# Three bursts of small-tile matmuls per batch in an attention and gated feed-forward kernel

## The chip, the cores and the metric

The kernel runs on one core of a Trainium2 chip, as one launch. The metric is the device time in microseconds. Five engines work side by side, each through its own queue in order: TensorE (PE in the profile; its weight loads are shown as PEld), VectorE (DVE), ScalarE (ACT), GpSimd (POOL) and SyncE (SP). They meet only through semaphores. TensorE writes to PSUM, an on-chip memory of eight banks of 2 KB per partition, from which VectorE and ScalarE read; all other operands lie in SBUF. DMAs bring data from and to the main memory (HBM), and some of them transpose within SBUF on the way.

## The reference

There are two stages. The first is an attention over 8 batches, 8 heads, 576 rows and a head width of 64, with 32 packing queries `p` per head; the second is a feed-forward layer with a cosine gate over all 4608 rows of 512.

```python
p_packed = sm_attn(p, k, v)                # 32 rows per head: softmax(scale p k^T) v
out = sm_attn(q, p_packed, p_packed)       # softmax(scale q p_packed^T) p_packed
x = out, heads side by side                # (8*576) x 512
h = x @ w_in                               # 512 x 2048
g = h * cos(h)
result = g @ w_out                         # 2048 x 512
```

The matmuls run in bfloat16 with float32 sums.

## The kernel before, in words

The work is done batch by batch. For a batch `b` the kernel does, in this order:

- `s1`: scores of `p` against `k`, 16 small matmuls (64 rows by 32 columns of the array, form 64*32), and ScalarE's exponentials into `a1`.
- `a1_xbar` (a DMA transpose on SP's queue) or `a1_pe` (TensorE): `a1` transposed into `a1T`, of which there is one buffer.
- `pp`: `a1T` times `v`, 48 small matmuls (form 96*32), copied to `pp_sb` in two copies.
- `pp_T`: two full transposes of `pp_sb` and a copy to `ppT`, the packed keys.
- `ppw` with n = 0 to 3: `ppT` times a quarter of `w_in`, eight small matmuls (64*32) each, copied from PSUM to `PPW`. This folds the second attention's values into `w_in`, so that `h` is computed from the 256 normalised weights `a2n` per row and not from `x`.
- `s2`: scores of `q` against the packed keys (16 small matmuls, 64*32), exponentials into `a2u`; `sums2`: their sums over heads by two full matmuls for each half; `normalise`: `a2n`.
- a slot: 16 steps, one for each 128 columns of `h`. Step `fc` is `h_mm` (four full matmuls of 288 columns, L254), the cosine on ScalarE (`cosT`, L258) and the product on VectorE (`gT`, L261).
- the output: `gT` times `w_out`, 16 matmuls of 512 columns (L342) for each of four chunks of 128 rows, and a fifth chunk (`joint`) for the last 64 rows of two batches; then a copy to `osb` and a store on SP's queue.

The order is written out by hand. The output matmuls of the batch before are the filler: `out_gen` yields after each of them, `fill(n)` issues the next n, so they stand between the dependent pieces and keep TensorE busy while other engines work. `set_filler(b)` (L353) first issues all that is left of the old batch. `slot` (L480) shares out the filler over its 16 steps, by weights, and keeps back `keep` of them; `hooks` are pieces inserted behind a given step, and a step in `heavy` gets half of its larger share ahead of its hook and half behind.

PSUM has three double-bank buffers (`psA`) that all of these share in turn, and two banks (`ot`) for the output. A piece that takes a `psA` buffer waits until the reader of the piece three takes earlier is done. `h_mm` uses 288 of the 512 columns in each bank of its buffer.

In the steady part (batches 3 to 6) the small tiles of a batch come in four bursts: `s2(s)` with `ppw(s, 2)`; `s1(s+1)` with `ppw(s, 3)`; `pp(s+1)` in slot `s` behind step 5, with `pp_T(s+1)` behind step 6; `pw2(s+1)`, that is `ppw(s+1, 0)` and `(s+1, 1)`, behind step 10. Slot 2 has `ppw(2, 2)`, `ppw(2, 3)`, `pp(3)` and `pw2(3)` behind four different steps. Between slots 1 and 2 stand `s1(2)`, `a1_pe`, `pp(2)`, `pp_T(2)`, `s1(3)`, `s2(2)`.

Three queues matter besides TensorE's. SP's queue carries the stores of the output, the transposes of `a1`, `q` and `k`, each in program order. POOL's queue carries the loads of `v`, `q` and `k`; a tiny copy from the transposed `k` (`gate`) ahead of a batch's loads holds them until that transpose has landed. VectorE's and ScalarE's queues are in program order too.

Of the kernel before, what the change touches and what calls it, by code (L numbers as in the profile page):

```python
# [15 lines left out]
def kernel(  # L16
# [15 lines left out]
    NFC = DF // 128  # L32
# [56 lines left out]
    def psa(dt=FP32):  # L89
        return psum["A"].tile([128, 2, 512 if dt == FP32 else 1024], dt, name="psA", tag="A")  # L90
# [104 lines left out]
    def ppw(b, n, eng=None, own=False, later=False, cuts=((0, 512),)):  # L195
        if b not in PPW:
            PPW[b] = ppw_pool.tile([128, 2, DF], BF16, name="PPW", tag="PPW")
        two = isinstance(eng, tuple)
        if own:
            ps = [bank(), bank()]  # L200
        else:
            t = psa()
            ps = [t[:, 0, :], t[:, 1, :]]
        for x in range(4):
            for y in range(2):
                r = slice(64 * y, 64 * y + 64)
                nc.tensor.matmul(ps[y][32 * x:32 * x + 32, :], ppT[b % 2][r, 0, x, :],  # L207
                                 w_in_bf[r, x, n * 512:(n + 1) * 512], start=True, stop=True)

        def evacuate(cuts=cuts):  # L210
            if own or two:
                for a, z in cuts:
                    for y in range(2):
                        copy(eng[y] if two else eng, PPW[b][:, y, n * 512 + a:n * 512 + z], ps[y][:, a:z])
            else:
                copy(eng or (V, ACT)[n % 2], PPW[b][:, :, n * 512:(n + 1) * 512], t)
        if later:
            return [lambda c=c: evacuate((c,)) for c in cuts]
        evacuate()
# [25 lines left out]

    gT, joint = {}, {}

    def h_mm(b, fc):
        if fc == 0:
            g_tile(b)  # L250
        ps = psa()
        for y in range(2):
            for e in range(2):
                nc.tensor.matmul(ps[:, e, 0:HS], PPW[b][:, y, fc * 128:(fc + 1) * 128],  # L254
                                 a2n[b][:, y, e * HS:(e + 1) * HS], start=(y == 0), stop=(y == 1))
        cs = cos_pool.tile([128, S], BF16, name="cosT")
        csv = cs.rearrange("p (e x) -> p e x", e=2)
        ACT.activation(out=csv, in_=ps[:, :, 0:HS], func=AF.Sin, bias=PI_HALF)  # L258

        def rest():  # L260
            V.tensor_tensor(out=gT[b][:, fc, :].rearrange("p (e x) -> p e x", e=2),  # L261
                            in0=ps[:, :, 0:HS], in1=csv, op=ALU.mult)
            if fc % 8 == 7:
                j0 = (b % 2) * 64
                G.tensor_copy(out=joint[b // 2][:, fc - 7:fc + 1, j0:j0 + 64],  # L265
                              in_=gT[b][:, fc - 7:fc + 1, 512:576])
        return rest
# [21 lines left out]
    def h_rest(b):  # L289

        t = psa()
        for fc in range(NFC):
            for y in range(2):
                nc.tensor.matmul(t[:, fc // 8, (fc % 8) * 64:(fc % 8) * 64 + 64],
                                 PPW[b][:, y, fc * 128:(fc + 1) * 128], a2n[b][:, y, 512:576],
                                 start=(y == 0), stop=(y == 1))
        cs = cos_pool.tile([128, 2, 512], BF16, name="cosR", bufs=1)
        ACT.activation(out=cs, in_=t, func=AF.Sin, bias=PI_HALF)
        j0 = (b % 2) * 64
        V.tensor_tensor(out=joint[b // 2][:, :, j0:j0 + 64],  # L300
                        in0=t.rearrange("p a (f x) -> p (a f) x", x=64),
                        in1=cs.rearrange("p a (f x) -> p (a f) x", x=64), op=ALU.mult)
# [16 lines left out]
    def n_chunks(b):  # L319
        return 5 if b % 2 and b < B - 1 else 4  # L320
# [13 lines left out]
    def out_gen(b):  # L334
        groups = [(0, 1), (2,), (3,)] if b == 0 else [(c,) for c in range(n_chunks(b))]
        for grp in groups:
            pss = {c: O.tile([128, DM], FP32, name="ot", tag="ot") for c in grp}
            for f0 in range(0, NFC, 4):
                for c in grp:
                    for fc in range(f0, f0 + 4):  # L340
                        w = joint[b // 2][:, fc, :] if c == 4 else gT[b][:, fc, c * 128:(c + 1) * 128]
                        nc.tensor.matmul(pss[c], w, w_out_bf[:, fc, :],  # L342
                                         start=(fc == 0), stop=(fc == NFC - 1))
                        if fc == NFC - 1:
                            osb = o_pool.tile([128, DM], FP32, name="osb")
                            copy(osb_eng[0], osb, pss[c])
                            for a, z, rows in pieces_of(b, c):
                                nc.sync.dma_start(out=rows, in_=osb[a:z, :])
                        yield

    filler = [None, 0]

    def set_filler(b):  # L353
        fill(1000)
        filler[0] = out_gen(b)
        filler[1] = 16 * n_chunks(b)

    def fill(n):
        while n > 0 and filler[1] > 0:
            next(filler[0])  # L360
            filler[1] -= 1
            n -= 1

    def load_w_in(n):
# [112 lines left out]
    rest_ppw()  # L477
    fill(7)

    def slot(s, hooks, keep=0, heavy={}):  # L480
        left = filler[1] - keep
        weight = [1 + heavy.get(fc, 0) for fc in range(NFC)]
        for fc in range(NFC):
            h_mm(s, fc)()
            quota = (left * sum(weight[:fc + 1])) // sum(weight) - (left + keep - filler[1])
            first = quota
            while hooks and hooks[0][0] == fc:
                if first == quota and fc in heavy:
                    first = quota // 2
                    fill(first)  # L490
                hooks.pop(0)[1]()
            fill(quota - first if first != quota else quota)

    def pw2(b, n=0, eng=None):
        ppw(b, n, eng)
        ppw(b, n + 1, eng)

    def tk(n, b, i):
        return lambda: pe_T(n, b, (ACT, V, ACT), (i,))

    def cross(n, b):
        return lambda: xbar(n, b)

    osb_eng[0] = ACT
    slot(1, [(2, lambda: ppw(1, 2, (ACT, V))), (4, lambda: h_rest(0)),
             (5, lambda: ppw(1, 3, (ACT, V))), (6, lambda: pack_p(2, 4)), (8, tk("k", 2, 0)), (9, tk("k", 2, 1)),
             (9, cross("q", 2)), (10, tk("k", 2, 2)), (12, cross("k", 3))], 4, {4: 2})
    ACT.preload_act_table_set(EXP_SET)
    osb_eng[0] = V
    G.tensor_copy(out=gate, in_=xT["k", 3][0:1, 0, 0:1])  # L510
# [1 line left out]
    load("q", 3)  # L512
    load("k", 4)

    fill(1000)
    set_filler(1)
    s1(2)
    fill(7)
    a1_pe(2, (0,))
# [2 lines left out]
    recips(2)  # L522
    fill(5)
    pp(2)
    fill(2)
    pp_T(2)
    s1(3)
    a1_xbar(3)
    recips(3)
    fill(6)  # L530
    s2(2)
    ppw(2, 0, V)
    xbar("q", 3)
    xbar("k", 4)
    fill(1)
    sums2(2, 0)
    fill(3)
    sums2(2, 1)
# [8 lines left out]
    for n, b in (("v", 4), ("q", 4), ("k", 5)):  # L547
        load(n, b)
    fill(9)
    osb_eng[0] = ACT  # L550
    slot(2, [(3, lambda: ppw(2, 2, (ACT, V))), (6, lambda: ppw(2, 3, (ACT, V))),
             (7, lambda: pp(3, ACT)), (8, lambda: pp_T(3, ACT)), (11, lambda: pw2(3))], 5, {11: 3})

    for s in range(3, B):
        nxt = s + 1 < B
        ACT.preload_act_table_set(EXP_SET)
        osb_eng[0] = V
        fill(1000)
        set_filler(s - 1)
        s2(s)  # L560
        ppw(s, 2, V)
        fill(8)
        if nxt:
            s1(s + 1)
            ppw(s, 3, V)
            a1_xbar(s + 1)
            xbar("q", s + 1)
            recips(s + 1)
            if s + 2 < B:
                xbar("k", s + 2)  # L570
                G.tensor_copy(out=gate, in_=xT["k", s + 2][0:1, 0, 0:1])
        else:
            ppw(s, 3, V)
        fill(4)
        sums2(s, 0)
        fill(5)
        sums2(s, 1)
        normalise(s)
        ACT.preload_act_table_set(SIN_SET)
        fill(13)  # L580
        osb_eng[0] = ACT
        for n, b in (("v", s + 2), ("q", s + 2), ("k", s + 3)):
            if b < B:
                load(n, b)
        slot(s, [(5, lambda: pp(s + 1, ACT)), (6, lambda: pp_T(s + 1, ACT)), (10, lambda: pw2(s + 1))] if nxt else [], 5, {10: 3})
    set_filler(B - 1)
    fill(1000)
    tail_chunk(B - 1, 4)
# [30 lines left out]
```

## Time and profile before

| | |
|---|---|
| median of 3 runs | 249.94 us (249.64 to 250.2) |
| the profiled execution | 249.57 us, its span 247.8 us |
| granted TensorE clock | 0.997 |
| TensorE busy | 238.0 us, 96% |
| ScalarE busy | 170.0 us, 69% |
| VectorE busy | 158.2 us, 64% |
| GpSimd busy | 38.1 us, 15% |
| output matmuls (L342), 512 columns | 560, 380 ns each |
| `h` matmuls (L254), 288 columns | 448, 286 ns each |
| `cosT` (L258), `gT` (L261) | 112 each, 652 and 756 ns |
| PPW copy of 1024 columns | 1222 ns on VectorE, 1012 ns on ScalarE |
| transposed `a1` by DMA | 5, from issue to landing 3.9 to 13.9 us |

The span runs from the first to the last instruction; the time of the execution holds 1.8 us more around it. The length of one matmul is longer than the distance between the starts of two, because matmuls are pipelined: sums are made with the distances. An engine is idle where its next instruction waits, and the profile names what ended last. The slots lie at about 40 to 62 us (slot 1), 75 to 94 (2), 104 to 120 (3), 129 to 148 (4), 158 to 173 (5), 183 to 201 (6) and 211 to 225 (7).

### The profile page before, as it was taken

The numbers are of one execution on the slowest core, as the hardware profiler recorded it, in microseconds if no ns is written. First come the engines' busy times: TensorE is split into PE (matmuls) and PEld (weight loads), VectorE is DVE, ScalarE is ACT, GpSimd is POOL, SyncE is SP. The second block draws the span as 40 slices with busy tenths as digits, with TensorE's granted clock in tenths as the row PEclk, the third lists the DMA queues.
The fourth block names the chain that finished last, engine by engine and source line by source line (L and its number), as shares of the span: only waits on it lengthen the run. The fifth ranks groups of instructions, "written<-read, shape, count | busy, mean of one in ns | idle before, by whom it ended". The sixth has DMA issues, their size and how long they took to land.

```text
span 247.8 us, 5456 instructions
## 1 busy us (share of the span) xinstructions
PE 238.0 (96%) x2239; PEld 128.3 (52%) x2239; DVE 158.2 (64%) x244; ACT 170.0 (69%) x284; POOL 38.1 (15%) x61
## 2 busy tenths in 40 slices
PE   7999899999999899999999999999999999999993
PEld 3463344566435554565446554565456554665452
DVE  3369987676449677578757666578756685774000
ACT  2359998667477777888787677977886685874110
POOL 8532320200130032004100500030000000000000
PEclk9999999999999999999999999999999999999998
DMA  6999999998799989996999796979592113111123
GB/s 91 205 209 209 202 207 228 198 238 144 160 128 184 201 188 186 213 208 170 177 177 233 128 228 143 176 148 182 115 184 62 42 45 84 43 33 54 52 75 85
DMA packets 63992, 37.37 MB, mean 151 GB/s; under 512 B 36592, under 2 KB 59376, under 8 KB 63968
## 3 DMA queue, kind: packets, MB, share of 16 engines
q0 software_dynamic: 23184, 18.81, 50.1%
q1 hardware_dynamic: 40624, 18.09, 35.5%
q8 instruction: 17, 0.28, 0.5%
q10 hardware_dynamic: 160, 0.13, 0.2%
q14 instruction: 7, 0.06, 0.1%
HBM read 37.22 MB, written 9.44 MB: 188 GB/s over the span
## 4 chain that ended last, share of the span: by engine, by line
PE 80%; ACT 5%; DVE 4%; issue 1%; DVEq 0%; ACTq 0%
PE ot L342 48%; PE psA L254 21%; PE psA L207 3%; PE psA L137 2%; ACT cosT L285 2%; PE psA L233 2%; DVE gT L286 1%; PE ot L328 1%; PE psA L180 1%; DVE PPW L87 1%; ACT cosT L258 1%; DVE gT L261 1%; ACT a2u L225 1%; DVE joint L300 0%; PE psA L192 0%
## 5 line engine op out<-in xcount | busy, mean ns | idle before, releaser
L342 PE MATMUL ot<-w_out_bf,gT 128*128 128x512 bf16 x512 | 133.2, 380 | 0.0
L261 DVE TENSOR_TENSOR gT<-psA,cosT 128x576 bf16<-128x576 f32 x112 | 83.5, 756 | 33.2 <-ACT cosT L258 32.2
L258 ACT ACTIVATE cosT<-psA 128x576 bf16<-128x576 f32 x112 | 72.9, 652 | 26.7 <-PE psA L254 25.3
L254 PE MATMUL psA<-a2n,PPW 128*128 128x288 bf16 x448 | 73.3, 286 | 0.1
L342 PEld LDWEIGHTS <-gT 128*128 128x128 bf16 x512 | 47.2, 98 | 43.4 <-issue 7.8
L254 PEld LDWEIGHTS <-PPW 128*128 128x128 bf16 x448 | 43.8, 98 | 30.8 <-issue 1.2
L87 DVE CAST PPW<-psA 128x1024 bf16<-128x1024 f32 (+1 forms) x25 | 26.1, 1048 | 6.8 <-PE psA L207 6.8
L87 DVE COPY osb<-ot 128x512 f32<-128x512 f32 (+1 forms) x14 | 9.4, 670 | 21.3 <-PE ot L328 17.4
L85 ACT COPY osb<-ot 128x512 f32<-128x512 f32 (+1 forms) x23 | 13.2, 576 | 13.5 <-PE ot L342 12.4
L265 POOL COPY joint<-gT 128x512 bf16<-128x512 bf16 x14 | 8.6, 616 | 85.3 <-DVE gT L261 85.2
L243 DVE SCALAR_TENSOR_TENSOR a2n<-a2u,r,lns 128x576 bf16<-128x576 bf16 x16 | 12.4, 813 | 8.2 <-ACT lns L241 8.2
L146 ACT ACTIVATE a<-psA 128x576 bf16<-128x576 f32 x16 | 10.3, 646 | 8.3 <-PE psA L137 8.3
L235 ACT ACTIVATE lns<-psA 128x576 f32<-128x576 f32 x16 | 10.3, 650 | 6.5 <-PE psA L233 5.9
L342 PE MATMUL ot<-w_out_bf,joint 128*128 128x512 bf16 x48 | 12.8, 379 | 0.0
L225 ACT ACTIVATE a2u<-psA,rs 128x576 bf16<-128x576 f32 x16 | 11.0, 736 | 1.0 <-PE psA L137 0.9
L379 PE MATMUL ot<-wz 128*128 128x512 bf16 (+1 forms) x17 | 9.0, 639 | 1.9 <-DVE wz L393 1.7
L207 PE MATMUL psA<-w_in_bf,ppT 64*32 64x512 bf16 x224 | 10.4, 380 | 0.0
L241 ACT ACTIVATE lns<-lns 128x576 f32<-128x576 f32 x16 | 10.0, 673 | 0.0
L286 DVE TENSOR_TENSOR gT<-psH,cosT 128x512 bf16<-128x512 f32 x15 | 9.3, 681 | 0.4 <-ACT cosT L285 0.4
L85 ACT CAST PPW<-psA 128x1024 bf16<-128x1024 f32 (+1 forms) x9 | 7.4, 826 | 2.9 <-PE psA L207 2.8
L285 ACT ACTIVATE cosT<-psH 128x512 bf16<-128x512 f32 x15 | 8.4, 627 | 0.7 <-DVE gT L286 0.6
L280 PE MATMUL psH<-a2n,PPW 128*128 128x512 bf16 x30 | 7.8, 382 | 0.8 <-DVE PPW L87 0.8
(94 smaller groups left out, 167.3 us busy)
## 6 DMA issues: line engine op xcount, KB each, us to landing
kbf<-in_k_dram POOLq DMA_DIRECT2D x8, 576.0 KB, 13.7
vbf<-in_v_dram POOLq DMA_DIRECT2D x8, 576.0 KB, 8.0
qbf<-in_q_dram POOLq DMA_DIRECT2D x8, 576.0 KB, 11.1
out_dram<-osb SPq DMA_DIRECT2D x24, 192.0 KB, 3.0
out_dram<-osb SPq DMA_DIRECT2D x22, 128.0 KB, 2.6
w_in_bf<-in_moe_w_in_dram POOLq DMA_DIRECT2D x4, 512.0 KB, 16.5
w_out_bf<-in_moe_w_out_dram POOLq DMA_DIRECT2D x4, 512.0 KB, 21.3
out_dram<-osb SPq DMA_DIRECT2D x26, 64.0 KB, 2.1
```

The costliest lines, as they stand in the source:

```text
L85: ACT.copy(out=out, in_=in_)
L87: eng.tensor_copy(out=out, in_=in_)
L146: ACT.activation(out=a1[b % 2][:, y, :, 0:TP].rearrange("p (e m) x -> p e m x", e=2), in_=ps[y][:, :, 0:HS].rearrange("p e (m x) -> p e m ...
L207: nc.tensor.matmul(ps[y][32 * x:32 * x + 32, :], ppT[b % 2][r, 0, x, :], w_in_bf[r, x, n * 512:(n + 1) * 512], start=True, stop=True)
L225: ACT.activation(out=a2u[b][:, y].rearrange("p (e x) -> p e x", e=2), in_=ps[y][:, :, 0:HS], func=AF.Exp, scale=rs1[b][:, y:y + 1])
L243: V.scalar_tensor_tensor(out=a2n[b][:, y], in0=a2u[b][:, y], scalar=r1[b][:, y:y + 1], in1=lns[b][:, y], op0=ALU.mult, op1=ALU.mult)
L254: nc.tensor.matmul(ps[:, e, 0:HS], PPW[b][:, y, fc * 128:(fc + 1) * 128], a2n[b][:, y, e * HS:(e + 1) * HS], start=(y == 0), stop=(y == 1))
L258: ACT.activation(out=csv, in_=ps[:, :, 0:HS], func=AF.Sin, bias=PI_HALF)
L261: V.tensor_tensor(out=gT[b][:, fc, :].rearrange("p (e x) -> p e x", e=2), in0=ps[:, :, 0:HS], in1=csv, op=ALU.mult)
L285: ACT.activation(out=cs, in_=ps, func=AF.Sin, bias=PI_HALF)
L286: return lambda: V.tensor_tensor(out=gT[b][:, fc, 0:512], in0=ps, in1=cs, op=ALU.mult)
L342: nc.tensor.matmul(pss[c], w, w_out_bf[:, fc, :], start=(fc == 0), stop=(fc == NFC - 1))
```

## The change

- In slot 1 `ppw(1, 2)` and `ppw(1, 3)` stand together behind step 2 (`pw2`), no longer behind steps 2 and 5; five outputs, not four, stand on each side of `h_rest`.
- `pp(2)` and `s1(3)` stand together, `pp_T(2)` behind them after three outputs; the outputs around `s2(2)` and `sums2(2)` are spread anew.
- In slots 2 to 6 one hook remains, `tiled(s)`, behind step 6 (slot 2) or 5: `ppw(s, 2)`, `ppw(s, 3)` and `pp(s+1)` in one burst. `pp` writes its 128 columns into the spare columns of the step's own buffer (`spare`); its copies, and those of `ppT`, go to VectorE. Most of the step's outputs stand ahead of the burst, three behind.
- `ppw(s, 0)` and `ppw(s, 1)` move from the slot before to `s2(s)` and `s1(s+1)`; for the last batch `ppw` 1 to 3 stand together.
- `pp_T(s+1)` moves behind the last step's `h_mm`, ahead of that step's `gT`.
- The filler becomes a list: what a slot leaves over (5, 10 or 13 outputs) is no longer issued at once but goes on ahead of the next batch's; so odd and even batches get about the same number of outputs per slot.

```diff
     def h_mm(b, fc):
         if fc == 0:
             g_tile(b)
         ps = psa()
+        spare[0] = ps[:, 1, HS:512]
...
-    filler = [None, 0]
+    filler = []
 
     def set_filler(b):
-        fill(1000)
-        filler[0] = out_gen(b)
-        filler[1] = 16 * n_chunks(b)
+        filler.append([out_gen(b), 16 * n_chunks(b)])
...
-    def slot(s, hooks, keep=0, heavy={}):
-        left = filler[1] - keep
-        weight = [1 + heavy.get(fc, 0) for fc in range(NFC)]
+    def slot(s, hooks, keep=0, heavy={}, last=None):
+        left = to_do() - keep
+        weight = [1 + heavy.get(fc, (0, 0))[0] for fc in range(NFC)]
         for fc in range(NFC):
-            h_mm(s, fc)()
...
+            rest = h_mm(s, fc)
+            if fc == NFC - 1 and last:
+                last()
+            rest()
+            quota = (left * sum(weight[:fc + 1])) // sum(weight) - (left + keep - to_do())
+            behind = min(quota, heavy[fc][1]) if fc in heavy else quota
+            fill(quota - behind)
             while hooks and hooks[0][0] == fc:
...
                 hooks.pop(0)[1]()
+            fill(behind)
...
+    def tiled(b):
+        own, later = spare[0], []
+        for n in (2, 3):
+            later += ppw(b, n, (ACT, V)[n - 2], later=True)
+        later[0]()
+        pp(b + 1, V, own=lambda: own)
+        later[1]()
...
-    slot(1, [(2, lambda: ppw(1, 2, (ACT, V))), (4, lambda: h_rest(0)),
-             (5, lambda: ppw(1, 3, (ACT, V))), (6, lambda: pack_p(2, 4)), ...], 4, {4: 2})
+    slot(1, [(2, lambda: pw2(1, 2, (ACT, V))), (4, lambda: h_rest(0)), (6, lambda: pack_p(2, 4)),
+             ...], 4, {2: (1, 2), 4: (3, 5)})
...
     pp(2)
-    fill(2)
-    pp_T(2)
     s1(3)
     a1_xbar(3)
+    fill(3)
+    pp_T(2)
     recips(3)
-    fill(6)
+    fill(5)
     s2(2)
...
-    slot(2, [(3, lambda: ppw(2, 2, (ACT, V))), (6, lambda: ppw(2, 3, (ACT, V))),
-             (7, lambda: pp(3, ACT)), (8, lambda: pp_T(3, ACT)), (11, lambda: pw2(3))], 5, {11: 3})
+    slot(2, [(6, lambda: tiled(2))], 10, {6: (5, 3)}, lambda: pp_T(3, V))
...
         s2(s)
-        ppw(s, 2, V)
+        ppw(s, 0, V)
         fill(8)
         if nxt:
             s1(s + 1)
-            ppw(s, 3, V)
+            ppw(s, 1, V)
...
         else:
-            ppw(s, 3, V)
-        fill(4)
+            for n in range(1, 4):
+                ppw(s, n, V)
+        fill(4 if nxt else 6)
...
-        slot(s, [(5, lambda: pp(s + 1, ACT)), (6, lambda: pp_T(s + 1, ACT)), (10, lambda: pw2(s + 1))] if nxt else [], 5, {10: 3})
+        if nxt:
+            slot(s, [(5, lambda: tiled(s))], 5 if s % 2 else 13, {5: (5, 3)}, lambda: pp_T(s + 1, V))
+        else:
+            slot(s, [], 5)
```

More of the change, by code (lines that the diff above doesn't have):

```diff
@@ L246 @@
     gT, joint = {}, {}
+    spare = [None]
     def h_mm(b, fc):
@@ L349, in out_gen, with to_do @@
                         yield
-    filler = [None, 0]
+    filler = []
     def set_filler(b):
-        fill(1000)
-        filler[0] = out_gen(b)
-        filler[1] = 16 * n_chunks(b)
+        filler.append([out_gen(b), 16 * n_chunks(b)])
+    def to_do():
+        return sum(n for _, n in filler)
     def fill(n):
-        while n > 0 and filler[1] > 0:
-            next(filler[0])
-            filler[1] -= 1
+        while n > 0 and filler:
+            next(filler[0][0])
+            filler[0][1] -= 1
+            if filler[0][1] == 0:
+                filler.pop(0)
             n -= 1
@@ L478, with pw2 @@
     fill(7)
-    def slot(s, hooks, keep=0, heavy={}):
-        left = filler[1] - keep
-        weight = [1 + heavy.get(fc, 0) for fc in range(NFC)]
+    def slot(s, hooks, keep=0, heavy={}, last=None):
+        left = to_do() - keep
+        weight = [1 + heavy.get(fc, (0, 0))[0] for fc in range(NFC)]
         for fc in range(NFC):
-            h_mm(s, fc)()
-            quota = (left * sum(weight[:fc + 1])) // sum(weight) - (left + keep - filler[1])
-            first = quota
+            rest = h_mm(s, fc)
[5 more added lines that the diff above has]
+            fill(quota - behind)
             while hooks and hooks[0][0] == fc:
-                if first == quota and fc in heavy:
-                    first = quota // 2
-                    fill(first)
                 hooks.pop(0)[1]()
-            fill(quota - first if first != quota else quota)
-    def pw2(b, n=0, eng=None):
+            fill(behind)
+    def pw2(b, n, eng=None):
         ppw(b, n, eng)
         ppw(b, n + 1, eng)
+    def tiled(b):
[5 more added lines that the diff above has]
+        later[1]()
     def tk(n, b, i):
@@ L504 @@
     osb_eng[0] = ACT
-    slot(1, [(2, lambda: ppw(1, 2, (ACT, V))), (4, lambda: h_rest(0)),
-             (5, lambda: ppw(1, 3, (ACT, V))), (6, lambda: pack_p(2, 4)), (8, tk("k", 2, 0)), (9, tk("k", 2, 1)),
-             (9, cross("q", 2)), (10, tk("k", 2, 2)), (12, cross("k", 3))], 4, {4: 2})
+    slot(1, [(2, lambda: pw2(1, 2, (ACT, V))), (4, lambda: h_rest(0)), (6, lambda: pack_p(2, 4)), (8, tk("k", 2, 0)), (9, tk("k", 2, 1)),
+             (9, cross("q", 2)), (10, tk("k", 2, 2)), (12, cross("k", 3))], 4, {2: (1, 2), 4: (3, 5)})
     ACT.preload_act_table_set(EXP_SET)
@@ L513 @@
     load("k", 4)
-    fill(1000)
     set_filler(1)
+    fill(4)
     s1(2)
@@ L534 @@
     xbar("k", 4)
-    fill(1)
+    fill(3)
     sums2(2, 0)
@@ L557 @@
         osb_eng[0] = V
-        fill(1000)
         set_filler(s - 1)
+        fill(5)
         s2(s)
-        ppw(s, 2, V)
+        ppw(s, 0, V)
         fill(8)
```

## The prediction

> **What bounds the kernel now.** I read the page's busy line and its chain first, then TensorE's timeline, then the DMA rows of one tile. The page:
>
> ```profile
> span 247.8 us, 5456 instructions
> PE 238.0 (96%) x2239; PEld 128.3 (52%) x2239; DVE 158.2 (64%) x244; ACT 170.0 (69%) x284; POOL 38.1 (15%) x61
> ...
> PE 80%; ACT 5%; DVE 4%; issue 1%; DVEq 0%; ACTq 0%
> ```
>
> TensorE is the bound and no other engine is near it. So the change must be priced in TensorE's time: what its instructions cost each other, and its waits. Starts of equal neighbours give the first: an output matmul (L342, 512 columns) follows the next by 0.216 us, an L254 (288 columns) by 0.122, so one step of a slot (four L254) is 0.49 us. The timeline of TensorE shows what a burst of small tiles adds (columns: start, length, work):
>
> ```profile
> 140.48 1.24 PE L342 MATMUL ot<-w_out_bf,gT 128*128 128x512 bf16 x5
> 141.66 0.62 PE L207 MATMUL psA<-w_in_bf,ppT 64*32 64x512 bf16 x16
> 142.21 0.61 PE L342 MATMUL ot<-w_out_bf,gT 128*128 128x512 bf16 x2
> ```
>
> Five outputs from 140.48 end their turns at 141.56; the burst starts at 141.66, an entry of 0.093 (the same for every burst that waits for nothing). From there to the next output are 0.558 us for 16 small matmuls, and 0.342 for eight (82.14 to 82.48). So eight cost 0.216 and leaving costs 0.126; the output after a burst is 0.010 late. One burst costs 0.093+0.126+0.010 = 0.229 us beyond its own matmuls. From 35 us on there are 31.
>
> The other cost is waiting. Gaps beyond these starts, added up: slot 1 0.30 and 0.18 (49.1 and 50.0, the buffer of h_rest) and 0.33 (53.9); before slot 2 0.05, 0.08 and 0.38; slot 2 0.15, 0.09 and 0.89; slots 3 and 5 0.35 each; slots 4, 6 and 7 none. The largest stands ahead of pp(3):
>
> ```profile
> 82.93 0.65 PE L254 MATMUL psA<-a2n,PPW 128*128 128x288 bf16 x4
> 84.40 0.56 PE L180 MATMUL psA<-vbf,a1T 96*32 96x64 bf16 x48 [0.82 <-DVE PPW L87]
> 84.89 0.60 PE L342 MATMUL ot<-w_out_bf,gT 128*128 128x512 bf16 x2
> ```
>
> The row blames VectorE, but the rows of a1T between 60 and 90 us name the last arrival:
>
> ```profile
> L160 SPq DMA_TRANSPOSE a1T<-a x1: 4630/4630/4630, 70.5 to 70.5; - x1
> its engine sat idle before it (us, times) until:
> ...
>   DMA a1T<-a: 1.1, 1
> ...
> DMA to landing us min/median/max: 13.9/13.9/13.9
> ```
>
> Issued at 70.45, landed 13.91 later at 84.36: pp(3) waits for a DMA, which TensorE's savings do not speed up. The sum is therefore split there.
>
> **Up to pp(3).** Slot 1: one burst joined (ppw 2 and 3), -0.229. With five outputs instead of four behind h_rest and no ppw ahead of pack_p, I count 0.06+0.06 left of 0.30+0.18, and 0.37 instead of 0.33 at the second kT transpose (its buffer still waits for ScalarE's 0.80 copy). s1(2) comes at 62.46 instead of 63.01.
>
> pp(2) then starts at 66.85 and issues its 48 in 0.358. s1(3) behind it would start at 67.2, but needs kT(3), whose transpose landed at 67.46 after a chain of loads that TensorE does not pace. I take 67.50 (was 68.67). It ends after 0.381; three outputs 0.648, pp_T 0.112 (its pp_sb was ready at 67.8), five outputs 1.08 and an entry put s2(2) at 69.81 (was 70.44). Three outputs instead of one cover a2u, which needs 1.18 after s2's start: 0.60+0.65 = 1.25, so the 0.38 goes. Slot 2 begins at 75.02 (was 75.57, with two outputs fewer done).
>
> In slot 2 VectorE is late: after a2n it still has two PPW copies and an osb, ending 1.98 after the slot's start, and the first gT is done at +2.64. With 1, 1, 2 outputs step 3 wants its buffer at +2.33: a wait of 0.36. Step 6 comes at +5.03, its own 0.49, six outputs 1.30, an entry 0.093 and sixteen ppw 0.432 later pp(3) wants to start: 75.02+5.03+2.31 = 82.36, say 82.45 with the change of shape below.
>
> Its a1T is issued 1.78 after s1(3), at 69.3 instead of 70.45, and now ahead of two output rows on SP's queue. In the trace's packets nothing of the SP queues moves from 69 to 73 us, while the loads of batches 3 and 4 start; then come the output rows; a1T's packets run from 74.9, one for one with the loads', 185 per us, about 100 per us beside output rows. There are 1536. Starting at 73 they are through by 82; starting 1.1 earlier than now, by 83.2. Landing between 82.2 and 83.3; I take pp(3) at 82.9. The bounds are 82.45 (no wait) and 84.40 (as now). The two output rows go out some 4.6 us later; four osb buffers of about 3.5 us each cover that. The gain here: 84.40-82.9 = 1.50.
>
> **From pp(3) on.** By then the new kernel has done three outputs more (0.65) and one step less (0.49): 0.16. The burst of ppw(3) in slot 2 is gone: 0.229. Slots 3 to 6 have one burst less each, but in the joined one the ppw tiles (64*32) meet those of pp (96*32). No row shows such a meeting. M, its cost, lies between 0 (s2 into ppw, both 64*32: 371+342-588 ns is the 0.125 of one exit) and 0.229 (as if the burst had been left). I take 0.1, the half that an entry is: 4 x (0.229-0.1) = 0.52. (The same meetings in slot 2 and at s1(3) hide under the two DMA waits.)
>
> The Trainium skill speaks against the joining: TensorEngine Tiling (Array Packing), Key Properties, says that a change of tiling mode, not of the tile alone, drains TensorE. It gives no figure; by it a joined burst of two shapes is still two drains, and were a drain a whole exit and entry, the 0.52 would be 0.
>
> The waits of slots 3 and 5 go (0.35+0.35): pp moves into the step's own buffer, pp_T to the slot's end. New there: pp_T takes the buffer of step 13, freed 2.2 us after that step's start (cosT 0.65, gT 0.76 and their starts), and wants it at 2.0 to 2.3: 0.19 in slot 2, 0.08 in slot 3. Net -0.43.
>
> What I cost at nothing, with its cover. The new step 6 shares its buffer with pp: pp ends 0.56 after its start, VectorE's two pp_sb copies take 0.42 more, and the step starts 0.49+0.01+0.65 after pp: some 0.13 spare, given by the three outputs behind the burst. If VectorE is late by x there, x is paid in five slots. PPW 3, behind pp_sb on VectorE (1.22), is done at 2.2 and needed at 3.0. pp itself waits for the step's gT, 2.3 after the step's start at worst; it wants to start at 2.3 (slot 3) to 2.7. ppT (0.29 on VectorE, ahead of the last gT) has 1.6 us until s2. pp_sb and ppT leave ScalarE, which is not the bound. In slot 7 three PPW copies of 1.22 queue on VectorE behind an osb: done 4.3, 5.5 and 6.6 after s2's start; sums2 wants the first two buffers at 4.5 and 5.8, step 0 the third at 8.9. POOL's queue keeps its order. a1T(4) landed at 108.15 for a pp(4) at 108.78; the new pp(4) is due near 107.6, and its a1T is issued 3 us earlier: 0 to 0.5, taken as 0.
>
> **Sum.** 1.50+0.16+0.23+0.52+0.43 = 2.84 us off the profiled execution's 249.57 us: 246.7. The runs shown have a median of 249.94, 0.37 above it, so 247.1.
>
> **The rivals.** (a) a1T(3) lands as now, at 84.4: the loads, not its issue, set it. For it: it landed 0.2 after kbf's load (84.16). Then only what follows pp(3) is gained, 1.34: 248.6. (b) No drain between small shapes and a1T in time: 0.45+0.40 more: 246.2. (c) The change of shape costs a whole burst, M = 0.23, and VectorE's slack of 0.13 at pp_sb is gone: -0.52 and some 0.2 in each of four slots: 248.4; with (a) 249.9, no change. (d) Slower: M beyond 0.81, in slots 3 to 6 (2.84+0.40 over four); at M = 1.0 the time is 250.7. For it only that no row shows the meeting; against it that no entry, exit or entry of 96*32 from 128*128 (0.093) is over 0.13. That the change does not do what it says is excluded by the order of TensorE's instructions: 22 bursts from 35 us on, not 31.
>
> **How the numbers follow.** Forecast 246.5 to 247.7: 0.50. (a) 0.22, (b) 0.11, (c) alone 0.08, both 0.04, (d) 0.05. 247.1 is the likeliest. The range from 246.0 to 248.9 takes in (b), (a) and (c), and leaves out 1 in 10. Within 0.2% (0.5 us, about what a measurement here can tell) is (c) with (a). Faster 0.90, same 0.05, slower 0.05.
>
> **What would show it.** Right: 22 bursts; pp behind ppw starting 0.43+M after it (M read directly); pp(3) between 82.4 and 83.3; a1T(3) issued near 69.3; no gap at the step after pp; slots 3 and 5 without gaps. Wrong: pp(3) still at 84.4; M over 0.2; gaps at the step behind pp with VectorE's pp_sb as releaser; a wait of sums2 in slot 7; new waits for a1T in slots 3 to 6.

## The result, and the profile after

The changed kernel takes 247.46 us (median of 17 runs, 246.26 to 250.19) against 249.78 us (17 runs) for the kernel before: a ratio of 0.9907, 95% interval 0.9891 to 0.9923, that is 2.3 us gained (1.9 to 2.7) where 2.84 were forecast. The profiled execution took 247.53 us against 249.57. (The ratios leave out executions more than 1.5% above the fastest of their kernel, which are one of the changed kernel's (250.19 us), one of run 3's (254.87) and three of run 9's six (251 to 255); what made them long was not traced.)

The first lines of the page, and its chain by engine:

```profile
span 245.7 us, 5424 instructions
PE 232.0 (94%) x2204; PEld 128.4 (52%) x2239; DVE 162.4 (66%) x259; ACT 166.6 (68%) x267; POOL 38.1 (16%) x61
...
PE 80%; DMA 13%; ACT 2%; issue 2%; DVE 1%; DVEq 0%
```

TensorE is still the bound, but the chain now holds 13% of DMA. About 7% is the first load of `q`; 6% is this transfer, as the rows of `a1T` between 60 and 90 us have it (operation, its issue; then from issue to landing):

```profile
L160 SPq DMA_TRANSPOSE a1T<-a x1: 4942/4942/4942, 69.2 to 69.2; - x1
...
DMA to landing us min/median/max: 14.4/14.4/14.4
```

and here is what waits for it, on TensorE's timeline of slot 2:

```profile
81.86 0.63 PE L207 MATMUL psA<-w_in_bf,ppT 64*32 64x512 bf16 x16
83.68 0.56 PE L180 MATMUL psA<-vbf,a1T 96*32 96x64 bf16 x48 [1.20 <-DMA a1T<-a]
84.39 0.59 PE L345 MATMUL ot<-w_out_bf,gT 128*128 128x512 bf16 x2 [0.16 <-issue]
```

pp(3) came at 83.68 instead of 84.40, a gain of 0.72. TensorE was ready for it 1.2 us earlier: it had been made faster than the transfer. (The last row's 0.16 is no wait: an output matmul is missing from the records there, as in all bursts marked so.)

The other reading is the meeting of the two small shapes, in slot 4, where nothing waits for a DMA:

```profile
134.13 0.62 PE L207 MATMUL psA<-w_in_bf,ppT 64*32 64x512 bf16 x16
134.68 0.55 PE L180 MATMUL psA<-vbf,a1T 96*32 96x64 bf16 x48
...
135.83 0.65 PE L257 MATMUL psA<-a2n,PPW 128*128 128x288 bf16 x4
```

Sixteen ppw take 0.432; pp starts 0.55 after the first of them. The meeting costs M = 0.12. It is the same in slots 3, 5 and 6. From 35 us on there are 22 bursts, as forecast, where there were 31. After pp(3) TensorE's last matmul comes 157.79 later, before it was 159.07: 1.28 gained there (forecast 1.34).

So two things had to be tried: whether 0.12 is really the price of a change of shape, and what makes a1T(3) land so late.

### The profile page after: what moved, and what is told of

It reads as the page before. It is cut to its first block, busy times and chain, and to the rows that moved or that the text cites. A ratio compares the mean times of both kernels' runs of the same rounds, so it can differ in the third digit from the quotient of the medians.

```text
span 245.7 us, 5424 instructions
## 1 busy us (share of the span) xinstructions
PE 232.0 (94%) x2204; PEld 128.4 (52%) x2239; DVE 162.4 (66%) x259; ACT 166.6 (68%) x267; POOL 38.1 (16%) x61
## 4 chain that ended last, share of the span: by engine, by line
PE 80%; DMA 13%; ACT 2%; issue 2%; DVE 1%; DVEq 0%
PE ot L345 45%; PE psA L257 21%; DMA qbf<-in_q_dram 7%; DMA a1T<-a 6%; PE ot L385 3%; PE psA L207 2%; PE psA L137 2%; PE psA L180 1%; PE ot L331 1%; PE psA L233 1%; PE psA L112 1%; ACT kT L85 1%; ACT a L146 1%; PE psA L192 0%; PE psA L170 0%
## 5 line engine op out<-in xcount | busy, mean ns | idle before, releaser
L345 PE MATMUL ot<-w_out_bf,gT 128*128 128x512 bf16 x483 | 127.3, 379 | 2.5 <-issue 2.1
L264 DVE TENSOR_TENSOR gT<-psA,cosT 128x576 bf16<-128x576 f32 x112 | 83.3, 757 | 19.5 <-ACT cosT L261 18.5
L345 PEld LDWEIGHTS <-gT 128*128 128x128 bf16 x512 | 48.1, 98 | 39.8 <-issue 4.4
L87 DVE CAST PPW<-psA 128x1024 bf16<-128x1024 f32 (+1 forms) x25 | 26.9, 1092 | 6.6 <-PE psA L207 6.4
L345 PE MATMUL ot<-w_out_bf,joint 128*128 128x512 bf16 x47 | 12.0, 380 | 0.2
L385 PE MATMUL ot<-wz 128*128 128x512 bf16 (+1 forms) x15 | 8.3, 660 | 2.0 <-DVE wz L399 1.7
L85 ACT CAST PPW<-psA 128x1024 bf16<-128x1024 f32 (+1 forms) x7 | 6.1, 891 | 5.8 <-PE psA L207 5.8
L207 PE MATMUL psA<-w_in_bf,ppT 64*32 64x512 bf16 x224 | 9.8, 379 | 0.0
L588 POOL COPY gate<-kT 1x1 bf16<-1x1 bf16 x3 | 0.5, 181 | 50.8 <-DMA kT<-kbf 50.8
## 6 DMA issues: line engine op xcount, KB each, us to landing
kbf<-in_k_dram POOLq DMA_DIRECT2D x8, 576.0 KB, 13.7
```

The costliest lines, as they stand in the source:

```text
L85: ACT.copy(out=out, in_=in_)
L87: eng.tensor_copy(out=out, in_=in_)
L345: nc.tensor.matmul(pss[c], w, w_out_bf[:, fc, :], start=(fc == 0), stop=(fc == NFC - 1))
L385: nc.tensor.matmul(wps, w[:, 0:128], w, start=True, stop=True)
```

## The experiments

All are edits of the changed kernel, each compared with the kernel before on its own chip. Since the first 35 us differ by up to 1.0 us from execution to execution, traces are compared from the start of s2(1) to the last matmul of TensorE ("from s2(1)"). Each row's last five columns are those of one traced execution. "Held" marks the runs whose loads wait until a1T(3) has landed.

| kernel | median us | ratio to before, 95% | from s2(1) | a1T(3), issue to landing | v(3)'s load issued ahead of a1T(3) by | a1T(3) lands behind k(4)'s load by | pp(3) waits for a1T(3) |
|---|---|---|---|---|---|---|---|
| before | 249.78 | | 208.35 | 13.91 | 2.70 | 0.20 | 0.82 |
| changed | 247.46 | 0.9907 (0.9891–0.9923) | 206.30 | 14.41 | 1.61 | 0.69 | 1.20 |
| 1 shapes mixed | 252.58 | 1.0108 (1.0078–1.0139) | 211.15 | 13.53 | 1.98 | 0.19 | 0.54 |
| 2 bursts apart | 248.07 | 0.9918 (0.9887–0.9949) | 206.81 | 13.90 | 2.12 | 0.72 | 0.62 |
| 3 loads behind a1T(3) | 252.53 | 1.0096 (1.006–1.0132) | 211.19 | 4.31 | held | | 0 |
| 4 outputs ahead | 246.78 | 0.9887 (0.9861–0.9912) | 205.31 | 14.67 | 1.54 | 0.66 | 0 |
| 5 four more | 248.62 | 0.9962 (0.9944–0.9981) | 207.60 | 14.60 | 1.54 | 0.35 | 0.52 |
| 6 six ahead | 246.81 | 0.9885 (0.9858–0.9913) | 205.29 | 12.83 | 2.96 | 0.43 | 0 |
| 7 behind two a1T | 254.46 | 1.0193 (1.0146–1.0241) | 212.14 | 4.33 | held | | 0 |
| 8 unequal outputs | 247.06 | 0.9903 (0.9872–0.9933) | 205.43 | 11.58 | 3.45 | 0.62 | 0 |
| 9 behind all a1T | 249.14 | 0.9886 (0.985–0.9922) | 205.19 | 4.61 | held | | 0 |
| 10 one behind | 248.59 | 0.9957 (0.993–0.9984) | 206.51 | 11.40 | 3.69 | 0.58 | 0 |
| 11 own buffer | 247.62 | 0.992 (0.9889–0.9952) | 206.95 | 13.94 | 2.03 | 0.66 | 0.73 |
| 12 three waits covered | 246.15 | 0.9881 (0.9856–0.9907) | 204.59 | 12.81 | 2.25 | 0.35 | 0 |

### What a change of shape costs: runs 1 and 2

Run 1 mixes the shapes, with `pp` cut into four pieces of twelve matmuls (its loop yields after every third `j`) and a piece taken after every four ppw:

```diff
-        for n in (2, 3):
-            later += ppw(b, n, (ACT, V)[n - 2], later=True)
+        small = pp(b + 1, V, own=lambda: own, parts=True)
+        for n in (2, 3):
+            later += ppw(b, n, (ACT, V)[n - 2], later=True, between=small)
...
+            if between is not None and x % 2:
+                next(between)
```

> The burst of slots 2 to 6 with the same 64 matmuls in another order: four of ppw, twelve of pp, and so on, so that the two shapes meet seven times and not once. Theory (every meeting of the two shapes costs TensorE 0.12 us, read from pp's start 0.55 after ppw's in the changed kernel): the burst of slots 3 to 6 grows from 1.05 to 1.77 us, 4 x 0.72 = +2.9; in slot 2 the wait for a1T(3) now comes after four ppw, so twelve ppw and six meetings, 1.0, lie behind it: +3.9 us in all, about 251.4. Rival (the 0.12 is one short wait of pp, for its buffer or its data, and not paid for each meeting): bursts as long as now, only slot 2 loses the twelve ppw, +0.3, 247.8.

TensorE's timeline of slot 4:

```profile
136.26 0.40 PE L215 MATMUL psA<-w_in_bf,ppT 64*32 64x512 bf16 x4
136.59 0.27 PE L186 MATMUL psA<-vbf,a1T 96*32 96x64 bf16 x12
136.79 0.40 PE L215 MATMUL psA<-w_in_bf,ppT 64*32 64x512 bf16 x4
137.12 0.27 PE L186 MATMUL psA<-vbf,a1T 96*32 96x64 bf16 x12
```

Each meeting is paid anew, in both directions. Twelve pp are a quarter of 0.358, 0.09, and the ppw behind them starts after 0.20: 0.11. The rival is dead. But a slot grew by 1.07 (from one s2 to the next 27.58 instead of 26.51), not 0.72. The four ppw show why: pp starts 0.33 behind them. With a meeting of 0.115, that is 0.216 for four, what eight take when they stand together. (In the changed kernel, too, pp starts 0.33 behind the second eight ppw, and these start 0.23 behind the first eight.) So cutting a group of eight in half saves nothing, and four half groups cost 0.43 in place of the reckoned 0; with six more meetings at 0.11 it is 1.1.

Run 2 takes the bursts apart. The edit moves three outputs from ahead of the burst to between ppw and pp; the three behind stay, unlike in the expectation, so that its wait of step 6 could not arise (run 10 has it).

```diff
-            fill(quota - behind)
+            fill(quota - behind - (3 if s >= 2 and fc in heavy else 0))
...
         later[0]()
+        fill(3)
         pp(b + 1, V, own=lambda: own)
```

> The changed kernel with the three outputs that stand behind ppw 2 and 3 and pp put between ppw and pp, in slots 2 to 6: bursts apart again, nothing else moved. Theory (a meeting costs 0.12, an exit and an entry 0.229): +0.11 in each of slots 3 to 6, and step 6 behind pp then wants its buffer 0.65 earlier, while pp_sb is ready 0.1 before it now: a wait of some 0.55 more in each, +2.6 in all; in slot 2 the outputs hide under the wait for a1T(3). Rival 1 (pp_sb is not what step 6 waits for): +0.4. Rival 2 (a meeting costs as much as a burst): no change, if the buffer is no limit either.

```profile
133.74 0.63 PE L207 MATMUL psA<-w_in_bf,ppT 64*32 64x512 bf16 x16
134.30 0.82 PE L345 MATMUL ot<-w_out_bf,gT 128*128 128x512 bf16 x3
135.05 0.56 PE L180 MATMUL psA<-vbf,a1T 96*32 96x64 bf16 x48
...
136.20 0.65 PE L257 MATMUL psA<-a2n,PPW 128*128 128x288 bf16 x4
```

From the burst's start to step 6 are 2.46, of which 0.648 are the three outputs between: 1.81 against 1.70 (134.13 to 135.83 above). Apart costs 0.11 a slot, as 0.229 less 0.12 says. So joining two shapes saves half of a burst, not a whole one and not nothing. Slots 4 to 6 lost 0.11 each; slot 3 lost more only because a1T(4) landed later in this execution (108.54).

### What makes a1T(3) late: runs 3, 5, 7 and 9

Run 3 holds the three loads that are issued just ahead of a1T(3) until it has landed:

```diff
-    load("v", 3)
-    load("q", 3)
-    load("k", 4)
...
     a1_xbar(3)
+    G.tensor_copy(out=gate, in_=a1T[3][0:1, 0, 0, 0:1])
+    load("v", 3)
+    load("q", 3)
+    load("k", 4)
```

> The loads of v(3), q(3) and k(4) are held on GpSimd's queue until a1T(3) has landed; in the changed kernel they are issued just ahead of it. Theory (a1T(3) lands 14.4 us after its issue because its packets take turns with those of the loads; alone the transposes of a1 of slots 5 and later take 4 to 5): a1T(3) lands near 74, pp(3) starts at 82.4 and not 83.68, 1.28 us gained there; v(3) lands near 80, in time. The loads of batch 4 then come some 3 to 5 us later and a1T(4) shares with them: it may land up to 4 late for pp(4) at 108.3. So 246.2 if a1T(4) is in time, up to 250 if not; in either case pp(3) at 82.4. Rival (the transfer is slow by itself, as the landing of a1T(3) was moved by 0.73 for an issue 1.23 earlier): pp(3) still at 83.5 or later, 247.5 or more.

The rows of `a1T`, first between 60 and 90 us, then between 92 and 125:

```profile
L160 SPq DMA_TRANSPOSE a1T<-a x1: 1437/1437/1437, 69.6 to 69.6; - x1
...
DMA to landing us min/median/max: 4.3/4.3/4.3
```

```profile
L160 SPq DMA_TRANSPOSE a1T<-a x1: 4815/4815/4815, 97.7 to 97.7; - x1
...
DMA to landing us min/median/max: 14.3/14.3/14.3
```

The theory holds: without the loads the transfer takes 4.3 us, and pp(3) starts 0.63 after its burst, with no wait for it. That is 0.08 more than in slots 4 to 6, because here the step's gT is late on VectorE: in runs 3, 8, 9 and 10 pp(3) starts 0.05 us behind the end of that gT. The same meeting then takes place one batch later, between a1T(4) and the loads that now come behind. This agrees with the Trainium skill, DMA: Bandwidth & Descriptors, Queues, rings and completion order: a DMA engine takes the queues that have work in turn, a packet at a time. In the trace of the changed kernel a1T's packets of 256 bytes run one for one with the loads' of 768, some 175 to 195 of each per us from 75 to 80 us.

That also tells when it lands. These are the rows of k(4)'s load, the last of the three, in the changed kernel and then in run 8 (see below), whose program is the same up to there:

```profile
L94 POOL DMA_DIRECT2D kbf<-in_k_dram x1: 772/772/772, 69.1 to 69.1; - x1
...
DMA to landing us min/median/max: 13.8/13.8/13.8
```

```profile
L94 POOL DMA_DIRECT2D kbf<-in_k_dram x1: 769/769/769, 67.7 to 67.7; - x1
...
DMA to landing us min/median/max: 12.9/12.9/12.9
```

In the changed kernel k(4) landed at 82.94 and a1T(3) at 83.63, in run 8 at 80.55 and 81.17. By the table a1T(3) landed 0.2 to 0.7 behind k(4) in all eleven executions where the loads run beside it, and was the longer under way the less the loads were ahead of it: 14.4 to 14.7 with v(3) issued 1.5 to 1.6 ahead, 11.4 and 11.6 with 3.7 and 3.5. The loads themselves go 0.3 after kT(3) has landed (at 67.33 and 65.85 here). That the landing follows the loads is read from these rows; only their removal was tried.

What followed was dearer than the wait. TensorE's timeline, and the windows of the same core (busy time of PE, PEld, DVE, ACT, POOL; then the granted clock):

```profile
106.96 0.62 PE L207 MATMUL psA<-w_in_bf,ppT 64*32 64x512 bf16 x16
112.08 0.83 PE L180 MATMUL psA<-vbf,a1T 96*32 96x64 bf16 x48 [4.50 <-DMA a1T<-a]
...
114.10 1.17 PE L257 MATMUL psA<-a2n,PPW 128*128 128x288 bf16 x4
```

```profile
107.00:112.00 5.00, 0.58 (x17) 0.09 (x16) 0.32 (x1) 1.01 (x1) 0.00 (x0) 0.98 1.29 178
112.00:115.50 3.50, 3.08 (x56) 1.96 (x58) 1.55 (x3) 0.20 (x1) 0.00 (x0) 0.54 1.19 154
115.50:120.00 4.50, 4.50 (x33) 2.94 (x31) 3.37 (x5) 3.86 (x7) 1.96 (x4) 1.00 0.91 221
```

After 4.5 us without work TensorE got half its clock. From s2(3) to s2(4) this kernel took 31.93, the changed one 25.93: 6.0, of which only 4.6 are the wait.

Run 7 also holds q(4) and k(5) behind a1T(4):

```diff
             a1_xbar(s + 1)
+            if s == 3:
+                G.tensor_copy(out=gate, in_=a1T[4][0:1, 0, 0, 0:1])
+                load("q", 4)
+                load("k", 5)
```

> The loads of v(3), q(3), k(4) behind the landing of a1T(3), as before, and now those of q(4) and k(5) behind the landing of a1T(4), with v(4) left ahead of it. Theory (each late a1T is late by the loads that it shares the DMA engines with, and no longer when they stand behind it): pp(3) at 82.4 without a wait; a1T(4), issued at 97.7, shares with v(4) alone and lands by 105, ahead of pp(4) at 107; q(4) and k(5) land near 110 and 114, in time: 1.28 gained on the changed kernel, 246.2. Rival (a transfer held back is late for its own reader): a wait at s2(4), s1(5) or pp(5) near 120 to 133, 246.8 to 249.

a1T(4) landed at 103.67, 5.4 after its issue, and pp(4) had no wait: right for the two that were freed. But neither theory nor rival had what came next. Batch 5's loads, issued from 119.8, met a1T(5), issued at 122.96, which took this long:

```profile
L160 SPq DMA_TRANSPOSE a1T<-a x1: 4911/4911/4911, 123.0 to 123.0; - x1
...
DMA to landing us min/median/max: 14.8/14.8/14.8
```

pp(5) waited 4.1 us, the clock was 0.51 for the six us behind it, and slot 4 was 7.0 longer (33.54 against 26.52).

Run 9 holds them in every batch: the edit of run 7 without its `if`, and only `v(s+2)` loaded ahead of the slot.

> As the two runs with loads held back, now for every batch: v(s+2) is loaded ahead as before, q and k behind the landing of that batch's a1T. The first held back one batch's loads and a1T(4) landed 14.3 us after its issue, the second two and a1T(5) landed 14.8 after: the meeting moved on by a batch each time. Theory (a1T is slow whenever three loads run beside it and takes 4 to 6 us beside none or one): all five land within 7 us of their issue, no pp waits, pp(3) at 82.4, and nothing else moves: 1.28 gained on the profiled execution of the changed kernel, 246.2. Rival (q and k are then late): waits of s2 or s1 in slots 5 to 7, over 247.

The five transfers landed 4.6, 6.0, 6.6, 6.1 and 7.7 after their issue, no pp waited, and the span from s2(1) was 205.19. So the mechanism is shown in every batch. Its last transfer took 0.7 longer than expected. As a kernel it is not to be had: half of its executions were 4 to 9 us longer. The loads of `q` and `k` now start some 13 us later, and their margins are thin (kT(6) landed at 146.44 for an s1(6) at 147.95); one that misses its reader would do that, but no such execution was traced, so the cause is open.

Run 5 asks whether the wait is TensorE's own. Four more output matmuls, whose result is not used, are put ahead of the burst in slot 2 and behind that of slot 4:

```diff
+                        if (b, c, fc) in ((1, 3, 0), (3, 3, 0)):
+                            for _ in range(4):
+                                nc.tensor.matmul(pss[c], w, w_out_bf[:, fc, :], start=True, stop=True)
                         nc.tensor.matmul(pss[c], w, w_out_bf[:, fc, :],
```

> Four more output matmuls (each a sum of its own into the bank that the chunk's first matmul then starts anew), 4 x 0.216 = 0.86 us of TensorE, at two places: in slot 2 just ahead of the burst with pp(3), and in slot 4 just behind the burst with pp(5). Theory (pp(3) waits 1.28 us for the landing of a1T(3), slot 4 has no wait): slot 2 absorbs its four, pp(3) still at 83.6 to 83.7 and slot 3 begins when it did; slot 4 pays 0.86 in full: +0.86 in all, 248.3. Rival (the 1.28 are paced by VectorE or by TensorE's own order, as the row ahead of the change blamed VectorE): pp(3) at 84.5, +1.7, 249.2.

```profile
80.59 1.03 PE L347 MATMUL ot<-w_out_bf,gT 128*128 128x512 bf16 x4
...
82.84 0.63 PE L207 MATMUL psA<-w_in_bf,ppT 64*32 64x512 bf16 x16
83.99 0.56 PE L180 MATMUL psA<-vbf,a1T 96*32 96x64 bf16 x48 [0.52 <-DMA a1T<-a]
```

Slot 2 swallowed most of its four: the burst came 0.98 later than in the changed kernel, pp(3) only 0.31, and that much later a1T(3) had landed (83.94 against 83.63). From one s2 to the next slot 2 grew by 0.20, slot 4 by 27.38 less 26.52 = 0.86, which is four starts of 0.216. With 0.24 lost ahead of s2(2), where s1(3) waited for kT(3), that is the 1.30 from s2(1). pp(3) is not paced by TensorE's own order, and VectorE, which the row of the kernel before blamed, is not what it waits for.

### Filling the wait: runs 4 and 6

```diff
-    slot(2, [(6, lambda: tiled(2))], 10, {6: (5, 3)}, lambda: pp_T(3, V))
+    slot(2, [(6, lambda: tiled(2))], 1, {6: (13, 3)}, lambda: pp_T(3, V))
...
-            slot(s, [(5, lambda: tiled(s))], 5 if s % 2 else 13, {5: (5, 3)}, lambda: pp_T(s + 1, V))
+            slot(s, [(5, lambda: tiled(s))], {3: 2, 4: 13, 5: 5, 6: 13}[s], {5: (5, 3)}, lambda: pp_T(s + 1, V))
```

That is run 4, which also has `fill(4)` and `fill(2)` around `sums2(1, 0)` and `(1, 1)` in place of 2 and 1. Run 6 has 4 and `{6: (10, 3)}` in slot 2 and leaves the start as it was.

> More outputs ahead of pp(3): slot 2 keeps 1 instead of 10 and sets the nine more of them ahead of its burst; slots 3 to 6 keep 2, 13, 5, 13; and four and two outputs instead of two and one stand around sums2 of batch 1, ahead of slot 1. Theory (pp(3) waits for the landing of a1T(3) at 83.6, whatever TensorE does before, so work moved ahead of it is free; the 1.2 us of waiting there hold five to six outputs of 0.216, and the three at the start cover part of the waits ahead of slot 1): 1.2 to 1.6 us gained, 245.9 to 246.3. Rival (the wait moves along with the work, as other engines pace it): no change, 247.5.

> The run with outputs set ahead of the wait again, without its three at the start and with six instead of nine in slot 2: slot 2 keeps 4 and not 10, slots 3 to 6 keep 2, 13, 5, 13. Theory: six of 0.216 are 1.30 and fill the wait of 1.28 ahead of pp(3) exactly; pp(3) at 83.7 with under 0.1 of wait; pp(4) then comes near 107.1 and waits up to 0.4 for a1T(4): 0.9 to 1.3 gained on the changed kernel, 246.2 to 246.6. Rival (the three outputs at the start were the useful ones): 247.0 or more.

Both gained 1.0 from s2(1) and 0.7 in the median, run 6 as expected on its trace, run 4 less. By the times alone that is not certain, as their intervals overlap the changed kernel's. Of the 0.65 of the three outputs at the start of run 4, 0.35 was left at s1(2), as the steps of slot 1 waited more, and 0.15 at s2(2), as s1(3) waited for kT(3); and run 4 lost that again in slot 3, to a1T(4) (0.22) and to pp_T (0.28 in place of 0.07). In run 6 pp(3) started at 84.16, 0.56 behind its burst, with a1T(3) landed at 82.51. Since it landed 1.1 earlier there than in the changed kernel's profile, the six were more than it needed: without their 1.30 pp(3) would have been due at 82.86, behind the landing. 0.18 came back as a wait in slot 3, whose first steps had fewer outputs. So it is run 4 that shows the filling: there a1T(3) landed at 84.63, pp(3) would have been due at 83.15 without its nine outputs, and started at 85.09 with no wait. In run 6 the gain at pp(3) came with the early landing, as in run 8, which fills nothing and is at 205.43 from s2(1).

### Where the waits of slots 3 and 5 went: runs 8, 10 and 11

Run 8 gives slots 3 to 6 a keep of 5 each. Run 11 calls `pp(b + 1, V)` without `own`.

> Slots 3 to 6 all keep 5 outputs, instead of 5, 13, 5, 13: slot 5 has eight outputs fewer than in the changed kernel, slot 4 eight more, slot 6 eight more and slot 7 eight fewer, as it was before the change; nothing else. Theory (the 0.35 of waiting in slot 5 went because pp no longer takes a buffer of its own, and because pp_T moved): slot 5 stays without a gap but for 0.1 to 0.3 at its shortest steps, 247.5 to 247.8. Rival (it went by the sharing): 0.35 or more back in slot 5, and some in slot 7, 247.9 to 248.3.

> pp takes a buffer of its own in turn again, and no longer the spare columns of the step's buffer; all else as changed. Theory of the prediction (the waits of 0.35 in slots 3 and 5 went because pp shares the step's buffer): 0.2 to 0.35 back in slots 3 and 5 at least, +0.4 to 0.7, 248.1. Rival (they went because pp_T moved to the slot's end and pp's copies to VectorE; the sharing of the outputs is excluded by the run with unequal outputs): no new gap, 247.5, or a little less, as step 6 no longer waits on pp_sb.

Run 8: slot 5, with eight outputs (1.73) fewer, took 25.03 instead of 26.51, so 0.25 more than its work, in two gaps of 0.18 and 0.07. The sharing is not it. It is also the run whose matmuls up to pp(3) are those of the changed kernel, with a1T(3) landing 11.58 after its issue:

```profile
82.23 0.63 PE L207 MATMUL psA<-w_in_bf,ppT 64*32 64x512 bf16 x16
82.86 0.55 PE L180 MATMUL psA<-vbf,a1T 96*32 96x64 bf16 x48
```

Run 11: slots 4 to 6 took 26.51, 26.52 and 26.51, as with the shared buffer; slot 3 was 1.02 longer, by the wait for a1T(4) alone. No gap came back, so the shared buffer, which the prediction named first, is not needed for it. The trace of the kernel before has the two places where slot 3 lost 0.14 and 0.16:

```profile
109.71 0.65 PE L254 MATMUL psA<-a2n,PPW 128*128 128x288 bf16 x4
110.34 0.27 PE L192 MATMUL psA<-ident,pp_sb 128*128 128x128 bf16 x2
...
116.15 0.38 PE L342 MATMUL ot<-w_out_bf,gT 128*128 128x512 bf16 x1
116.53 0.65 PE L254 MATMUL psA<-a2n,PPW 128*128 128x288 bf16 x4
```

One is pp_T, one step behind pp, waiting for pp_sb (110.34 where 110.20 was due); the other stands one step behind the two ppw (116.53 for 116.37). Both pieces left the middle of the slot. That they, not the buffer, carried the 0.30 is read from these rows; it was not tried by putting them back.

Run 10 takes away what the prediction named as cover of pp_sb, with `{5: (5, 1)}` in place of `{5: (5, 3)}` in slots 3 to 6.

> One output instead of three behind the burst in slots 3 to 6, two more ahead of it. Theory (step 6 shares its buffer with pp, and pp_sb's copies on VectorE end 0.09 before step 6 starts, so there is almost nothing to spare): step 6 wants to start 0.43 earlier and waits 0.35 to 0.4 in each of the four slots: +1.4 to 1.6, 249.0. Rival (the copies move forward with the matmuls, or the step has slack that the trace does not show): no change, 247.5.

```profile
135.37 0.39 PE L345 MATMUL ot<-w_out_bf,gT 128*128 128x512 bf16 x1
135.98 0.65 PE L257 MATMUL psA<-a2n,PPW 128*128 128x288 bf16 x4 [0.23 <-ACT PPW L85]
```

Step 6 was due at 135.59 and came 0.39 later; slots 3 to 6 grew by 0.27, 0.38, 0.27 and 0.39 (1.31 of the 1.4 to 1.6 expected). The row names ScalarE's copy, which ended at 135.93; VectorE's pp_sb ended then too (its next copy started at 135.94). By the order of the buffers it is pp_sb's; the run does not part the two.

### Three waits covered: run 12

```diff
             if fc == NFC - 1 and last:
+                fill(1)
                 last()
...
-             (8, tk("k", 2, 0)), (9, tk("k", 2, 1)), (9, cross("q", 2)), (10, tk("k", 2, 2)), (12, cross("k", 3))], ...
+             (8, tk("k", 2, 0)), (9, cross("q", 2)), (10, tk("k", 2, 1)), (12, tk("k", 2, 2)), (12, cross("k", 3))], ...
```

with the keeps of run 6.

> Six outputs ahead of the burst of slot 2 as before (keeps 4, then 2, 13, 5, 13), one output ahead of pp_T in a slot's last step, and the transposes of k(2) in slot 1 behind steps 8, 10 and 12 instead of 8, 9 and 10. Theory (each of these waits is one of an operation set too close behind its supplier): pp(3) waits for nothing, or little where a1T(3) lands late; the 0.07 to 0.14 ahead of pp_T in slots 2 to 4 go, 0.2 to 0.3 together; the 0.33 and 0.11 ahead of the second and third transposes in slot 1 go: 1.0 to 1.3 + 0.2 + 0.4 gained on the changed kernel's profiled execution, 245.6 to 246.0. Rival (the waits of slot 1 are VectorE's and ScalarE's pace, and come back at the next step): 246.2 to 246.6.

It takes 246.15 us, the least of all, and 204.59 from s2(1), 1.71 below the changed kernel: 1.2 at pp(3), 0.43 ahead of s2(2) and 0.20 at pp_T, less 0.18 in slot 3, is 1.65 of it. The waits of slot 1 did not come back at the next step. The 1.2 is not shown to be the outputs' doing in this execution: a1T(3) landed at 81.53, and without the six pp(3) would have been due at 81.91. The intervals of its ratio and of the changed kernel's overlap (from 0.9891 to 0.9907), so by the times alone it is likely, not certain, that it is faster; the trace shows each of the waits gone.

## Why the prediction was right, and where it was not

- **Faster, 2.84 forecast, 2.3 measured (2.04 between the two profiled executions).** The direction and the two-part split were right, and the likeliest case happened.
- **Up to pp(3): the term that was mis-sized.** The wish of TensorE was right to 0.05: pp(3) wanted to start at 82.49 (81.86 and the 0.63 of runs 3 and 8), forecast 82.45; a1T(3) was issued at 69.22, forecast 69.3. What failed is "landing between 82.2 and 83.3; I take pp(3) at 82.9": it landed at 83.63, and 0.72 was gained in place of 1.50. The step counted a1T's own packets from its own issue, and took one execution's landing for a fixed one. The traces tie it to the loads: it landed 0.2 to 0.7 behind k(4) each time, 11.40 to 14.67 after its issue (median 13.7 in the ten executions of the changed kernel and its edits), and the loads start with the landing of kT(3). The forecast's 13.6 is the middle of that, its range of 1.1 a third of it. In runs 8 and 10, whose program up to pp(3) is the changed kernel's, the loads were early and pp(3) came 47.41 after s2(1), against 48.52 in the changed kernel's trace and 49.27 before: a gain of 1.86 and not 0.75. So it was in part luck that the sum came as near as it did. How far the kernel before scatters is not known; it has one trace.
- **Rival (a)**, that the loads set the landing and not the issue, was nearer the mechanism than the sum: the loads it is (run 3, and the landing close behind k(4) in each trace). Its number, 84.4, did not come, because k(4) itself landed earlier than before (82.94, not 84.16).
- **Joining two shapes**: 0.10 taken, 0.12 measured in four slots, 0.11 to 0.12 in run 1 with seven meetings. The 0.52 became 0.44. Rivals (b), (c) and (d), which needed 0, 0.23 and over 0.81, are excluded. The rule on drains that stood against the joining is right that a change of mode costs, and run 2 puts the size at half of a burst.
- **Waits of slots 3 and 5**: gone as forecast, pp_T's new wait was 0.136 and 0.067 (0.19 and 0.08 forecast). The amount was right; the reason given first, the buffer, is not needed (run 11), and the second, that pp_T moved, fits the rows.
- **Costed at nothing**: pp's wait for the step's gT was 0.08 in slot 2 where a1T(3) was in time (run 8). The cover of pp_sb held (0.13 to spare by the forecast): in the changed kernel VectorE is done with it by 135.65, when its next copy starts, and step 6 starts at 135.83; run 10 shows the price when the cover is gone. No wait appeared in slot 7. pp(4) had no wait for a1T(4), which landed at 107.46 for a start at 108.32; in runs 2, 4 and 11 it did (up to 1.02), so that cover was thinner than "0 to 0.5, taken as 0" made it.

## What to carry to other kernels

Count what small tiles cost by their changes of shape: here 0.093 in, 0.126 out, 0.12 between two small shapes, and a group of eight tiles cut into fours costs as much per four as for eight. A transfer that shares the DMA engines with others has no length of its own: here it landed just behind the last load, whether the loads had been issued 1.5 or 3.7 us ahead of it. Before speeding up the engine that waits for it, look at its landing and theirs in several executions, and put work that is due anyway ahead of the wait (run 4). Holding back the loads handed the meeting to the next batch (runs 3 and 7), or left the loads' own readers little margin (run 9). Where a piece moved and its waits went, a run that moves back one part of it tells which part did it.

## What was not expected of the hardware

- One and the same transfer took 11.40 to 14.67 us from its issue, a spread of 3.3 us, more than the whole change is worth, while TensorE's distances repeat to 0.01. Counted from the first of the loads beside it, it landed after 15.0 to 16.2 us, a spread of 1.2.
- A wait of 4.1 to 4.5 us costs TensorE more than itself: the granted clock was 0.54 and 0.51 behind it. It came back 3.1 us after the restart in run 3 and 6.1 in run 7; by the clock's records it was at half for 3.42 us and for twice that, 6.83. The Trainium skill, TensorE: Matmul & The Clock Gate, Part 1: The HAM clock gate, says that an idle stretch of about 3.4 us halves the clock, which these runs agree with, and that full speed returns some 4 us into steady work, give or take half a microsecond; run 7's 6.1 is longer, and the measurement decides.
- Four 64*32 matmuls of 512 columns, followed by another shape, take 0.216 as eight do.
